# A linear-attention and feed-forward kernel on one core: new task lengths in its order planner, two small tiles moved to ScalarE, a ring of three, other PSUM banks at the end

## The chip, the cores and the metric

The kernel runs on one core of a Trainium2 chip. A core has four engines that compute: TensorE (PE, matmuls; the profile lists its weight loads apart as PEld), VectorE (DVE), ScalarE (ACT) and GpSimd (POOL). A fifth, SyncE (SP), issues the transfers (DMAs). Each engine works through its own queue strictly in the order in which the program was written, and waits at an instruction whose inputs or whose room are not there yet. The metric is the device time of one execution in microseconds (us); less is better.

## The reference

What is computed is a recurrence over 768 time steps, for 32 (batch, head) pairs with a state of 40 by 40, then a layer norm and a feed-forward block on its output:

```python
for t in range(S):                         # S = 768
    y[:, :, t] = einsum('bhd,bhde->bhe', rt, state)
    Sa = einsum('bhde,bhe->bhd', state, at)
    state_decay = state * wt[:, :, None, :] - einsum('bhd,bhe->bhde', Sa, bt)
    state = state_decay + einsum('bhd,bhe->bhde', vt, kt)
...
xn = (x - mu) / np.sqrt(var + 1e-06) * g_ln
ch = np.maximum(xn @ w_ch1, 0.0) @ w_ch2   # 320 -> 1280 -> 320
return x + ch
```

All of it is in float32.

## The kernel before

**Tiling.** The 768 steps are cut into 24 chunks of 32 steps (`NCH`, `C`). Inside a chunk the recurrence is written as matrices: a triangular system is set up (`prep`), its inverse is built (`invert` and `merge`), the state is carried to the next chunk (`chain`), and the chunk's output is formed (`post`). `norm` normalises a chunk's 128 output rows and transposes them; `moe` runs the feed-forward block over two chunks at a time (a pair, 256 rows). In `moe` the 1280 hidden units go in ten slices `f`: layer 1 of a slice is 8 matmuls of 256 columns into one PSUM bank (L794), ScalarE takes the rectified high part out into `hh` (L797), VectorE the remainder into `hl` (L799), and layer 2 is 6 matmuls of 320 columns that add to the pair's two output banks (L778). `weights` loads the feed-forward weights in pieces and converts each to a high and a low part, with work on ScalarE, VectorE (L671 to L674) and TensorE (L717, L718).

**The inverse.** The triangular blocks go through DRAM (`d_l`), come back one row per matrix (`yv`), and are inverted there by 14 pairs of small multiplications and additions (L425, L429): on VectorE for chunks 0 and 1, on GpSimd from chunk 2 on. The result goes through DRAM again (`d_h`) and comes back as `hv`. `merge(c)` multiplies `hv` twice by a column of 0 and 1 (`half`) into the tile `dg` (L444; block diagonals), on VectorE for chunks 0 and 1, on GpSimd after that, and two groups of matmuls (L452, L462) and a transposition (L472) make the full inverse `tt`, which `chain` needs (L531).

**The order of the work.** No line of the kernel issues work straight away. Each step is a task that is handed to the planner (`op`, `dma`, then `Plan.add`) with an engine, a length in us, a key (its priority, about the chunk's number), what it reads and writes, the PSUM banks it opens, and for transfers their KB. `Plan.order` then simulates the engines and goes on picking the task that can start soonest, on each engine the lowest key among those within 0.05 us, and issues the tasks in the order of the planned starts. The planned times are thrown away; only the order in each queue and the choice of banks stay. On the chip an engine waits if something planned to be there isn't.

The planner knows a few more things. `HOP` is added when a result passes between engines. A transfer goes through one pipe (`pipe`) at 200 KB per us, and the next is held until the pipe is at most `queue` us from free. On PE, `dense` tasks (the feed-forward block) and the other, `sparse` ones are alternated: after 2.9 us of sparse work (`SPARSE`) a dense task is wanted, and dense work goes on for at least 1.7 us (`DENSE`). Each PE task has a number of instruction records (`recs`); every 128 of them (`READ`) a fetch of 3.8 us (`FETCH`) must be through. Tasks with `lock=True` (scans and products on VectorE and GpSimd) are never planned at the same time.

PSUM has eight banks in three groups: A (four, the recurrence and the conversion of weights), H (two, layer 1, `norm`'s transposition and the first step of the conversion), M (two, the output of layer 2):

```python
with tc.manual_schedule():
    for t in P.order(dict(A=[0, 1, 2, 3], H=[4, 5], M=[6, 7])):
        t["fn"]()
```

`hh` and `hl` are rings of two tiles, so layer 1 of slice `f` may not be planned before layer 2 of slice `f - 2` is done (`room`, L796). Keys: `consts` makes `half` and `ones` (from the identity, L308 and L310) with key -60; `prep(0)` and `prep(1)` have -5.4 and -4.4, so those small operations come ahead of nearly all of `prep(0)` that is ready at the time.

Of the kernel before, what the change touches and what calls it, by code (L numbers as in the profile page):

```python
# [49 lines left out]
class Plan:  # L50


    HOP = 0.15
    SPARSE, DENSE = 2.9, 1.7
    READ, FETCH, STALL = 128, 3.8, 0.2
# [29 lines left out]
    def order(self, free):  # L85
# [13 lines left out]
        pipe, out, lock = 0.0, [], 0.0  # L99
# [19 lines left out]
        while len(out) < len(T):  # L119
            best = None  # L120
            for e, ns in ready.items():
# [17 lines left out]
                if best is None or s < best[0]:  # L139
                    best = s, n  # L140
# [7 lines left out]
            end = s + t["us"]  # L148
            if t["lock"]:
                lock = end  # L150
            if t["recs"]:
                read += t["recs"]
                if read >= self.READ:
                    read -= self.READ
                    at = end - t["us"] * read / t["recs"]
                    since = max(at, since + self.FETCH)
                    end += since - at
# [25 lines left out]
def body(ctx, tc, ea, eb, vr, rd, vt, w1, w1x_in, w2, gl, fe, fd, out):  # L183
# [62 lines left out]
    hh, hl = ring(2, "hh", 256, dt=F32R), ring(2, "hl", 256, dt=F32R)  # L246
# [18 lines left out]
    def dma(key, kb, rd, wr, to, of, us=0.4, queue=2.0):  # L265
# [4 lines left out]
    def consts():  # L270
# [40 lines left out]
        op("DVE", 1.5, -60, ["ident"], ["half", "ones"], f)  # L311
# [16 lines left out]
    def prep(c):  # L328
# [17 lines left out]
        op("DVE", 1.4, kp, W + [("start", h)], [("q", i)] + ([("go",)] if c == 0 else []), lambda: nc.vector.tensor_tensor_scan(  # L346
            out=flat(q[R])[:, ::-1], data0=t[R, n:0:-1], data1=flat(start[h][R])[:, ::-1], initial=0.0,
            op0=ALU.mult, op1=ALU.max), lock=True)
        op("DVE", 0.29, kp, [("q", i)], ["last"], lambda: nc.vector.reciprocal(
            out=last[R, :, 0:1], in_=q[R, :, 0:1]))  # L350
        op("DVE", 1.35, kp, W + ["last"], [("g", i)], lambda: nc.vector.tensor_tensor_scan(
            out=flat(g[R]), data0=t[R, 0:n], data1=flat(last[R]), initial=0.0, op0=ALU.mult, op1=ALU.max), lock=True)
        eng, e, us = ("DVE", nc.vector, 1.0) if c < EARLY else ("POOL", nc.gpsimd, 1.8)
        for hf, rs in enumerate(ROWS):
            if c >= XS:
                op("POOL", 0.6, kp - 0.3, (), [("x2k", x, 2 * hf), ("x2k", x, 2 * hf + 1)], lambda vs=slice(VROW[hf], VROW[hf] + C), hf=hf: nc.gpsimd.memset(
                    x2s[x][vs, hf, 0:512], 0.0))
            op(eng, 0.75 * us, kp, W + [("q", i)], [("x2a", x, hf)], lambda hf=hf, rs=rs: e.tensor_tensor(  # L358
# [6 lines left out]
        op(eng, 1.25 * us, kp, [("g", i)], K, lambda: e.tensor_tensor(  # L365
# [15 lines left out]
        for bb in range(2):  # L381
            m = 32 * j + 16 * bb
            dma(kp + 0.3, 150, [("gk", i)], [("d_l", s, 2 * j + bb)], d_l[s][m:m + 16].rearrange("m a t -> a m t"),
                gk[i][64 * bb + C:64 * bb + 64].rearrange("a (m t) -> a m t", t=C), 0.5)
        for hf in range(2):
            for bb in range(2):
                dma(kp + 0.4 + (1.0 if c < 2 else 0.0), 33, [("gk", i)], [("x2k", x, 2 * hf + bb)],
                    x2s[x][VROW[hf]:VROW[hf] + C, hf, 256 * bb:256 * bb + 256],
                    gk[i][64 * bb:64 * bb + C, 256 * hf:256 * hf + 256], 0.65)
# [10 lines left out]
        op("PE", 0.35, c - 1.8, ["qc", "ident"], [b], f, opens=[b], room=[("pi", c % KT)], recs=4)  # L400
        op("ACT", 0.45, c - 1.8, [b], [("pi", c % KT)], lambda b=b: nc.scalar.copy(
# [3 lines left out]
    def invert(s):  # L405
# [6 lines left out]
        eng, e, us = ("DVE", nc.vector, 0.54) if c0 < 2 else ("POOL", nc.gpsimd, 0.8)  # L412
# [3 lines left out]
        dma(k0, 131 * n // 32, L, Y, y[:, 0:1024], d_l[s].rearrange("m a t -> m (a t)"))  # L416
# [16 lines left out]
        dma(k0 + 0.4, 150 * n // 32, Y, [("d_h", s, 0)], d_h[s][:, :, B:3 * B].rearrange("a m t -> m a t"), rows[:, 0:B], 0.65)  # L433
        dma(k0 + 0.2, 150 * n // 32, L, [("d_h", s, 1)], d_h[s][:, :, 0:B].rearrange("a m t -> m a t"), d_l[s][:, B:C, 0:B], 0.65)

    def merge(c):
# [3 lines left out]
        dma(c - 1.3 - soon(c), 100, [("d_h", s, 0), ("d_h", s, 1)], [("hv", i)], hv[i],  # L440
            d_h[s][:, 32 * j:32 * j + 32].rearrange("a (g h) n -> g a (h n)", h=4), 0.6)
        eng, e = ("DVE", nc.vector) if c < 2 else ("POOL", nc.gpsimd)
        for x in range(2):
            op(eng, 0.25 if c < 2 else 0.4, c - 0.8 - soon(c), [("hv", i), "half"], [("dg", i)], lambda x=x: e.tensor_scalar(  # L444
                out=dg[i][:, :, :, x].rearrange("p y h t -> p h y t"),
# [553 lines left out]
```

## Time and profile before

| what | value |
|---|---|
| median of 3 runs | 575.66 us (572.37 to 577.28) |
| the profiled execution | 572.31 us |
| its span, first to last instruction | 570.2 us |
| mean granted TensorE clock | 0.969 |
| DMA over the span | 62.33 MB, 109 GB/s mean |

The span is what the profile shows; the profiled execution takes 2.1 us more than its span. In the tables of the profile, "idle before" is the time in which an engine did nothing ahead of an instruction, and the name behind the arrow is what ended the wait. "issue" there means that nothing the profile shows was waited for. "PEclk" is the granted clock of TensorE as a share of full speed. A window "A:B" is a stretch in us from the span's start. "x32" counts instructions.

### The profile page before, as it was taken

To read this page: it belongs to the slowest core of one execution; us is meant where nothing else is said; L and a number is where in the kernel's file an instruction comes from. 1 tells how busy PE (TensorE), PEld (TensorE's weight loads), DVE (VectorE), ACT (ScalarE), POOL (GpSimd) and SP (SyncE) were. 2 spreads that over 40 slices of the span, in tenths; PEclk is the share of its full clock that TensorE was granted. 3 is DMA by queue.
4 is the path that set the end of the run, shared out by engine and by line. 5 is a ranking of instruction groups with operands and counts; after the bars stand their busy time and mean duration, and the time that the engine had idled before them with its cause. 6 is when DMAs were issued, how large, how long until landed. Compare 5 with 4: busy or idle time off the path is not lost.

```text
span 570.2 us, 30783 instructions
## 1 busy us (share of the span) xinstructions
PE 504.1 (88%) x13462; PEld 452.9 (79%) x13462; DVE 404.0 (71%) x888; ACT 333.1 (58%) x848; POOL 304.1 (53%) x551
## 2 busy tenths in 40 slices
PE   2508787999999999999999999999999998999995
PEld 1406665798888898989888899899899897888995
DVE  7887897588638768767766774797884666778621
ACT  6538657674665765566556556666666656466321
POOL 9315277677284865864766836747838717200000
PEclk9999868699999999989999999999999999899999
DMA  6574665423533443443444344334434444333000
GB/s 165 130 203 126 173 184 160 117 79 109 130 86 102 121 126 86 107 114 89 102 131 103 89 114 110 103 101 110 126 81 108 115 100 115 100 108 95 3 24 28
DMA packets 80299, 62.33 MB, mean 109 GB/s; under 512 B 56224, under 2 KB 65440, under 8 KB 80160
## 3 DMA queue, kind: packets, MB, share of 16 engines
q1 hardware_dynamic: 80160, 60.31, 40.2%
q8 instruction: 107, 1.75, 1.3%
q14 instruction: 32, 0.26, 0.1%
HBM read 48.49 MB, written 9.44 MB: 102 GB/s over the span
## 4 chain that ended last, share of the span: by engine, by line
PE 58%; POOL 9%; issue 5%; DMA 4%; DVE 4%; ACT 3%; SPq 2%; POOLq 0%; DVEq 0%; ACTq 0%
PE bank L778 16%; PE bank L794 16%; POOL ytmp L425 3%; POOL yv L429 3%; PE bank L606 3%; PE bank L375 3%; PE bank L496 2%; PE bank L546 2%; PE bank L623 2%; PE bank L531 2%; PE bank L521 2%; PE bank L591 2%; PE bank L579 2%; SPq L266 1%; PE bank L472 1%
## 5 line engine op out<-in xcount | busy, mean ns | idle before, releaser
L778 PE MATMUL bank<-w,hh 128*128 128x320 f32 x480 | 116.5, 328 | 0.0
L794 PE MATMUL bank<-xh,w 128*128 128x256 f32 x480 | 107.9, 288 | 2.6 <-DVE hl L799 2.0
L797 ACT ACTIVATE hh<-bank 128x256 fp32r<-128x256 f32 x120 | 46.1, 384 | 96.8 <-PE bank L794 94.4
L799 DVE SCALAR_TENSOR_TENSOR hl<-bank,hh 128x256 fp32r<-128x256 f32 x120 | 50.1, 420 | 73.3 <-ACT hh L797 72.2
L794 PEld LDWEIGHTS bank<-xh,w 128*128 128x128 f32 x480 | 82.8, 190 | 4.3 <-DVE hl L799 2.4
L778 PEld LDWEIGHTS bank<-w,hh 128*128 128x128 f32 x480 | 76.6, 189 | 3.4
L778 PE MATMUL bank<-w,hl 128*128 128x320 f32 x240 | 74.6, 311 | 0.0
L365 POOL TENSOR_TENSOR bk<-bk,gE 104x1024 f32<-104x1024 f32 x22 | 50.9, 2313 | 32.7 <-DMA bk<-in_eb_dram 13.5
L794 PE MATMUL bank<-xl,w 128*128 128x256 f32 x240 | 67.6, 282 | 0.0
L358 POOL TENSOR_TENSOR x2s<-wa,qE 40x512 f32<-40x512 f32 x44 | 52.9, 1202 | 23.8 <-DVE qE L346 17.1
L425 POOL TENSOR_TENSOR ytmp<-yv 64x28 f32<-64x28 f32 (+6 forms) x154 | 55.5, 360 | 11.3
L429 POOL TENSOR_TENSOR yv<-yv,ytmp 64x28 f32<-64x28 f32 (+6 forms) x154 | 53.9, 350 | 12.1
L506 POOL MEMSET x5s<- 64x512 f32 x48 | 25.1, 523 | 48.3 <-PE bank L623 43.1
L501 ACT COPY xk<-bank 64x320 f32<-64x320 f32 x96 | 40.2, 419 | 17.7 <-PE bank L496 15.7
L612 DVE TENSOR_TENSOR x5s<-bank,mask 64x256 f32<-64x256 f32 x96 | 40.5, 422 | 13.6 <-PE bank L606 11.0
L794 PEld LDWEIGHTS bank<-xl,w 128*128 128x128 f32 x240 | 45.8, 191 | 0.0
L778 PEld LDWEIGHTS bank<-w,hl 128*128 128x128 f32 x240 | 45.6, 190 | 0.0
L535 ACT COPY x<-bank 32x320 f32<-32x320 f32 x96 | 40.1, 417 | 8.6 <-PE bank L531 7.2
L594 ACT COPY xk<-bank 40x320 f32<-40x320 f32 x96 | 40.2, 419 | 6.2 <-PE bank L591 4.3
L444 POOL TENSOR_SCALAR dg<-hv,half 128x128 f32<-128x128 f32 x44 | 29.6, 688 | 22.5 <-DMA hv<-d_h 22.5
L375 PE MATMUL bank<-x2s,bk 104*64 104x64 f32 x768 | 31.1, 240 | 11.4 <-issue 5.4
L475 ACT ACTIVATE tt<-bank,half 32x128 f32<-32x128 f32 x96 | 34.4, 358 | 10.6 <-PE bank L472 7.5
(136 smaller groups left out, 1130.9 us busy)
## 6 DMA issues: line engine op xcount, KB each, us to landing
wa<-in_ea_dram SPq DMA_DIRECT2D x48, 162.7 KB
bk<-in_eb_dram SPq DMA_DIRECT2D x48, 160.0 KB
vu<-in_vr_dram SPq DMA_DIRECT2D x48, 160.0 KB
wa<-in_ea_dram SPq DMA_DIRECT2D x24, 165.0 KB
x<-in_vt_dram SPq DMA_DIRECT2D x48, 80.0 KB
x5s<-in_rd_dram SPq DMA_DIRECT2D x48, 80.0 KB
out_dram<-ot SPq DMA_DIRECT2D x24, 160.0 KB
r<-in_w_dram SPq DMA_DIRECT2D x10, 320.0 KB
```

The lines of the kernel that those rows point to most:

```text
L358: op(eng, 0.75 * us, kp, W + [("q", i)], [("x2a", x, hf)], lambda hf=hf, rs=rs: e.tensor_tensor(out=x2s[x][rs, hf, 0:512].rearrange("p (h ...
L365: op(eng, 1.25 * us, kp, [("g", i)], K, lambda: e.tensor_tensor(out=kb, in0=kb, in1=g[R, :, 0:C].unsqueeze(2).broadcast_to([104, 16, 2, C] ...
L375: mm(pg[64 * bb:64 * bb + 64, :, h], lhsT=tb[R, 64 * p:64 * p + 64], rhs=x2s[x][R, :, 32 * p:32 * p + 32], start=True, stop=True)
L425: e.tensor_tensor(out=tv, in0=yb[:, :, j + 1:, j:j + 1].broadcast_to(S), in1=yb[:, :, j:j + 1, 0:j].broadcast_to(S), op=ALU.mult)
L429: e.tensor_tensor(out=v, in0=v, in1=tv, op=ALU.add)
L501: op("ACT", 0.45, c - 1.2 + 0.1 * bb, [bs[hf]], [X[hf]], lambda b=bs[hf], zs=zs, hf=hf, bb=bb: nc.scalar.copy(out=xk[i][zs, hf, 8 * bb:8 * ...
L594: op("ACT", 0.44, k + 0.35, [bs[hf]], [("ST", i)], lambda b=bs[hf], rs=rs, hf=hf, bb=bb: nc.scalar.copy(out=xk[i][rs, hf, 8 * bb:8 * bb + ...
L612: op("DVE", 0.46, k + 0.5, [b, "mask"], [("z", i)], lambda b=b, zs=zs, ps=ps, hf=hf, bb=bb: nc.vector.tensor_tensor(out=x5s[i][zs, hf, 8 * ...
L778: mm(bank_of(po[u])[:, 0:CH], lhsT=l[:, us], rhs=ws[f"w2_{f // 2}"][:, f % 2, x], start=f == 0 and n == 0, stop=f == 9 and n == 2)
L794: mm(ph, lhsT=l, rhs=r, start=n == 0, stop=n == 7)
L797: yield "ACT", 0.39, [phs[f]], [("hh", f % 2)], lambda f=f: nc.scalar.activation(out=hht[f % 2], in_=bank_of(phs[f])[:, 0:256], func=AF.Re ...
L799: yield "DVE", 0.46, [phs[f], ("hh", f % 2)], [("hl", f % 2)], lambda f=f: nc.vector.scalar_tensor_tensor(out=hlt[f % 2], in0=bank_of(phs[ ...
```

## The change

It has five parts.

1. **Lengths and rates of the planner.** Some forty task lengths are replaced by others, most within 10%: layer 1 from 1.0 to 1.03, layer 2 from 0.95 to 0.98, the scans from 1.4 and 1.35 to 1.28, the GpSimd products from 1.35 to 1.18 (L358), a converted slice of a weight from 1.5 to 1.56, the transfer of `d_l` from 150 to 113 KB, that of `vr` from 110 to 164. A PE task planned to start before 49.6 us now counts 1.8 times its length; after a planned gap of over 1.7 us on PE, tasks count 1.7 times for 3.4 us. The DMA pipe goes from 200 to 270 KB per us. `HOP` and `FETCH` are slightly smaller.
2. **Ties and locks.** Where two locked tasks on different engines could start at the same planned time, the one with the lower key is taken; before it was the engine listed first. GpSimd's `dg` products are now locked.
3. **The first diagonals.** In `merge(0)` and `merge(1)` the two products into `dg` are done by ScalarE. The products into `half` and `ones` get key -4.5 in place of -60.
4. **Rings of three.** `hh` and `hl` have three tiles each, so layer 1 of slice `f` needs layer 2 of slice `f - 3` to be done.
5. **Banks of the last pair.** The ten layer-1 results of the last pair of chunks go to group A in place of H.

```diff
-    HOP = 0.15
+    HOP, LAST = 0.13, 0.06
     SPARSE, DENSE = 2.9, 1.7
-    READ, FETCH, STALL = 128, 3.8, 0.2
+    READ, FETCH, STALL = 128, 3.75, 0.2
+    FIRST, COLD, WAIT, AFTER, LOW = 49.6, 1.8, 1.7, 3.4, 1.7
...
-                if best is None or s < best[0]:
+                if best is None or s < best[0] or s == best[0] and T[n]["lock"] and T[best[1]]["lock"] and T[n]["key"] < T[best[1]]["key"]:
                     best = s, n
...
-            end = s + t["us"]
+            us = t["us"]
+            if t["eng"] == "PE":
+                if s - engines["PE"] > self.WAIT:
+                    cold = max(cold, s + self.AFTER)
+                us *= self.COLD if s < self.FIRST else self.LOW if s < cold else 1.0
+            end = s + us
...
-            done = end
+            done = end + (self.LAST if t["eng"] == "PE" else 0.0)
             if t["eng"] == "SP":
-                pipe = max(pipe, end + 1.3) + t["kb"] / 200.0
-                done = pipe + 0.7 + t["late"]
+                pipe = max(pipe, s + 1.4) + t["kb"] / 270.0
+                done = pipe + 1.0 + t["late"]
...
-    hh, hl = ring(2, "hh", 256, dt=F32R), ring(2, "hl", 256, dt=F32R)
+    hh, hl = ring(3, "hh", 256, dt=F32R), ring(3, "hl", 256, dt=F32R)
...
-        op("DVE", 1.5, -60, ["ident"], ["half", "ones"], f)
+        op("DVE", 1.3, -4.5, ["ident"], ["half", "ones"], f)
...
+        sc = c < 2
         for x in range(2):
-            op(eng, 0.25 if c < 2 else 0.4, c - 0.8 - soon(c), [("hv", i), "half"], [("dg", i)], lambda x=x: e.tensor_scalar(
...
+            if sc:
+                op("ACT", 0.35, c - 0.8 - soon(c), [("hv", i), "half"], [("dg", i)], lambda x=x, to=to, of=of: nc.scalar.mul(
+                    out=to, in_=of, mul=half[:, x:x + 1]))
+            else:
+                op("POOL", 0.6, c - 0.8 - soon(c), [("hv", i), "half"], [("dg", i)], lambda x=x, to=to, of=of: nc.gpsimd.tensor_scalar(
+                    out=to, in0=of, scalar1=half[:, x:x + 1], scalar2=None, op0=ALU.mult), lock=True)
...
-            yield "PE", 1.0, X + W, [phs[f]], fn, [phs[f]], [(a, f % 2) for a in ("hh", "hl")]
+            yield "PE", 1.03, X + W, [phs[f]], fn, [phs[f]], [(a, f % R) for a in ("hh", "hl")]
...
-                    [out[2 * g], out[2 * g + 1]], bank_of, [Bank("M"), Bank("M")], [Bank("H") for _ in range(10)]):
+                    [out[2 * g], out[2 * g + 1]], bank_of, [Bank("M"), Bank("M")], [Bank("H" if c + 1 < NCH else "A") for _ in range(10)]):
```

The other changed lines replace a length or a number of KB. The number of operations and transfers, and what each computes, stays as it was, but for the four products that go from VectorE to ScalarE.

More of the change, by code (lines that the diff above doesn't have):

```diff
@@ L718, in f @@
                     mm(at(h), lhsT=minus, rhs=ws[tag][:, h, 0], start=False, stop=True)
-                op("PE", 0.75, key, M + W + ["ident", "minus", "diag"], [one[h]], f,
+                op("PE", 0.8, key, M + W + ["ident", "minus", "diag"], [one[h]], f,
                    opens=[one[h]] if k == 2 or h == 0 else (), recs=3)
             if k == 1:
-                op("ACT", 0.63, key, [one[0]], W, lambda: nc.scalar.copy(
+                op("ACT", 0.59, key, [one[0]], W, lambda: nc.scalar.copy(
                     out=ws[tag][:, :, 1], in_=bank[one[0].at].rearrange("p (k n) -> p k n", k=2)))
@@ L725, in pair @@
                 for h in range(2):
-                    op("ACT", 0.45, key, [one[h]], W, lambda h=h: nc.scalar.copy(out=ws[tag][:, h, 1], in_=at(h)))
+                    op("ACT", 0.43, key, [one[h]], W, lambda h=h: nc.scalar.copy(out=ws[tag][:, h, 1], in_=at(h)))
         last(0.0)
```

114 lines of the change are left out of this document (57 added, 57 removed).

## The prediction, made before the changed kernel had run

> **What bounds the kernel now.** I read the table of stages first, the busy time of each engine in six windows, because the page's shares mix a start, a long middle and an end.
>
> ```profile
> core 0: us, PE busy (x) PEld busy (x) DVE busy (x) ACT busy (x) POOL busy (x), PEclk, DMA share, GB/s
> 0.00:42.00 42.00, 11.45 (x253) 9.87 (x257) 35.48 (x104) 21.24 (x41) 20.24 (x42) 1.00 0.63 163
> 42.00:57.00 15.00, 13.23 (x430) 10.32 (x422) 11.36 (x14) 11.65 (x30) 9.06 (x6) 1.00 0.48 138
> 57.00:114.00 57.00, 46.13 (x906) 36.14 (x904) 44.61 (x90) 37.47 (x93) 34.15 (x64) 0.76 0.60 158
> 114.00:535.00 421.00, 404.77 (x11675) 368.44 (x11675) 301.62 (x653) 256.20 (x668) 240.60 (x442) 0.99 0.40 104
> 535.00:563.36 28.36, 28.34 (x218) 28.00 (x216) 10.31 (x28) 6.57 (x18) 0.00 (x0) 1.00 0.04 13
> 563.36:570.20 6.84, 0.19 (x2) 0.09 (x2) 0.66 (x3) 0.00 (x0) 0.00 (x0) 0.87 0.17 58
> ```
>
> From 114 us on TensorE (PE) is the bound: 404.77 of 421 us busy, then 28.34 of 28.36. Its work there is the same in any order, so a new order can win only the idle 16.2 us and what the clock loses. Before 42 us VectorE sets the pace (35.48 of 42), with PE waiting. Between 57 and 114 us nothing is full: PE idles 10.9 us, and its clock is granted at 0.76. Where that clock is lost:
>
> ```profile
> 77.50:87.50 10.00, 9.35 (x82) 7.16 (x81) 9.17 (x23) 6.82 (x17) 8.20 (x24) 0.52 0.67 181
> 98.00:111.50 13.50, 13.36 (x237) 9.79 (x234) 7.47 (x13) 8.10 (x21) 8.68 (x15) 0.52 0.57 155
> 244.50:248.50 4.00, 4.00 (x79) 3.73 (x79) 2.21 (x5) 2.80 (x8) 3.24 (x5) 0.61 0.58 155
> ```
>
> Two stretches at half clock early on; a short one later, right behind an idle 1.62 us (the 243.70 row below). Half clock doubles a group: the 32 matmuls of L375 take 1.98 us at 78.13 and 1.15 at 443.39.
>
> ```profile
> 75.16 0.69 PE L623 MATMUL bank<-xk,x5s 128*32 128x40 f32 x50 [1.65 <-issue]
> 78.13 1.98 PE L375 MATMUL bank<-x2s,bk 104*64 104x64 f32 x32
> 97.25 1.86 PE L375 MATMUL bank<-x2s,bk 104*64 104x64 f32 x32 [1.57 <-POOL bk L365]
> 243.70 0.34 PE L496 MATMUL bank<-ident,bk 40*64 40x40 f32 x9 [1.62 <-issue]
> 443.39 1.15 PE L375 MATMUL bank<-x2s,bk 104*64 104x64 f32 x32 [0.56 <-POOL bk L365]
> ```
>
> So a PE gap of about 1.6 us costs more than itself: 244.50 to 248.50 at 0.61 lost 4 x 0.39 = 1.6 us of work; the stretches from 77.5 and 98 lost 10 x 0.48 = 4.8 and 13.5 x 0.48 = 6.5, as far as PE was then the bound.
>
> **Step 1, the first diagonals go to ScalarE.**
>
> ```profile
> 38.93 1.26 DVE L346 TENSOR_TENSOR_SCAN qE<-wa,start 104x528 f32<-104x528 f32 x1
> 40.21 1.39 DVE L444 TENSOR_SCALAR dg<-hv,half 128x128 f32<-128x128 f32 x2
> 46.36 2.98 DVE L444 TENSOR_SCALAR dg<-hv,half 128x128 f32<-128x128 f32 x2
> 45.14 2.99 POOL L365 TENSOR_TENSOR bk<-bk,gE 104x1024 f32<-104x1024 f32 x1 [2.34 <-issue]
> 41.70 0.62 PE L452 MATMUL bank<-hv,dg 32*32 32x16 f32 x32 [14.80 <-DVE dg L444]
> 51.69 0.44 PE L452 MATMUL bank<-hv,dg 32*32 32x16 f32 x32
> 35.11 0.70 SPq L266 DMA_DIRECT2D hv<-d_h x1
> 209.40 4.30 DMA hv<-d_h
> L639 ACT ACTIVATE diag<-ident,gt 128x128 f32<-128x128 f32 x2 | 0.7, 394 | 0.0
> ```
>
> The row of L452 shows PE idle for 14.80 us until `dg(0)`. Removed from VectorE: 1.39 + 2.98 = 4.37 us. Added to ScalarE: four products like L639's, the same shape with a scale from a column: 4 x 0.394 = 1.58 us, the two of a chunk in 0.79. For `dg(0)`: `hv` was issued at 35.11, and by a later transfer's 4.30 us from there on it lands at about 35.81 + 4.30 = 40.1, just when VectorE starts. So only 1.39 - 0.79 = 0.6 us is won there, provided ScalarE's copy of `qc`, 0.63 us long and ready with the scan's end at 40.19, goes second; if first, the win is nothing. For `dg(1)`, 2.98 - 0.79 = 2.2 us, but PE reaches that L452 only at 51.69, behind the state of chunk 0, so this can be zero unless the planner moves it up. Besides, VectorE has 4.37 us less in a stretch that it fills. Bounds 0 to 4.4 us; I take 0.6 + 2.2 = **2.8**, because the early stage is a chain through VectorE and PE in turn, and `dg(1)` gates chunk 1.
>
> The 2.98 us overlap a GpSimd product (45.14 to 48.13), the 1.39 one at 40.27. The Trainium skill (SBUF — State Buffer, section "SBUF: two separate sides") says that VectorE and GpSimd share a port pair that one holds for a whole instruction, and that ScalarE never waits for it. By that rule the move takes the collision away; the two rows agree, and the sum already has it.
>
> **Step 2, `half` and `ones` with a later key.**
>
> ```profile
> 7.47 0.14 DVE L308 TENSOR_TENSOR ones<-ident 32x16 f32<-32x16 f32 x1
> 8.81 0.26 DVE L349 RECIPROCAL last<-qE 104x16 f32<-104x16 f32 x1
> 15.00 0.69 DVE L378 TENSOR_TENSOR gk<-bank,sign 128x512 f32<-128x512 f32 x1 [0.67 <-PE bank L375]
> 21.80 0.69 DVE L378 TENSOR_TENSOR gk<-bank,sign 128x512 f32<-128x512 f32 x1 [0.54 <-PE bank L375]
> ```
>
> They stand on VectorE from 7.47 to 8.8, ahead of all of chunk 0's products; moved back, chunk 0 is 1.3 us earlier. VectorE's work before 40 us is the same, so only its idle time can shrink: 0.67 + 0.54 = 1.2 us. Bounds 0 to 1.2; I take **0.7**. ScalarE's `lt` copies, which read `ones`, become ready later and hold nothing before `merge`.
>
> **Step 3, rings of three and step 5, other banks.**
>
> ```profile
> L794 PE MATMUL bank<-xh,w 128*128 128x256 f32 x410 | 92.7, 289 | 2.6 <-DVE hl L799 2.0 <-DVE xl L766 0.6
> ```
>
> Between 114 and 535 us layer 1 waited for `hl` 2.0 us in all. That wait can be the ring or the H bank that L799 frees; a third tile doesn't add a bank. Bounds 0 to 2.0; I take **0.5**. The last pair's banks: the window from 535 us has 0.02 us of idle PE, so there is nothing to fill, and I take 0; bounds 0 and, if copies of group A are in the way, one L799 wait like those above, 1 us lost.
>
> **Step 4, lengths, rates and ties: only order.** Nothing becomes shorter on the chip. What a better order can take away are PE's waits:
>
> ```profile
> PE bank L397 <- ACT qc L398: 2.0, 1, 2.0
> PE bank L623 <- issue: 1.7, 1, 1.7
> PE bank L375 <- POOL bk L365: 1.6, 1, 1.6
> PE bank L496 <- issue: 2.9, 2, 1.6
> PE bank L531 <- issue: 2.8, 2, 1.4
> PE bank L452 <- POOL dg L444: 1.5, 2, 1.0
> PE bank L531 <- ACT tt L475: 1.1, 1, 1.1
> ```
>
> The first three lie in 57:114, the rest in 114:535. In the middle, "issue" waits are the larger part: 2.9 and 2.8 of 16.2 us alone; the planner's fetch length moves only from 3.8 to 3.75, so I leave them. Waits for an engine add up to 7.2 us of the 10.9 early (nine rows, 2.0 to 0.2) and to 7.4 us of the 16.2 later (nine rows, 2.0 to 0.2). Changes of length are mostly under 10%; the large ones are true to the trace (half-speed PE at the start; GpSimd's `dg` 0.6 us in place of 0.4). The tie rule keeps GpSimd's inversions from going ahead of VectorE's scans in the plan. Ends: all 14.6 us won, or as much lost by new gaps; I take a fifth won, **3.0 us**, near nothing because the middle is already 96% busy.
>
> **The sum.** 572.3 (the profiled execution, whose span is 570.2) - 2.8 - 0.7 - 0.5 - 3.0 = 565.3, **565 us**. The profiled execution lies 3.4 us under the median, 575.66, so against that median the forecast is 1.9% faster. Within 1% means 569.9 to 581.4; a 1% change is about what a measurement of this kernel can tell from none, as three runs of it span 572.37 to 577.28.
>
> **The rivals.**
>
> *A, the half clock goes.* If the new order closes the gaps that end at 75.16 and 97.25, the stretches behind them stay at full clock: 4.8 + 6.5 = 11.3 us more, 565.3 - 11.3 = 554 us. For it: the planner now prices such gaps. Against: it picks the task that can start soonest either way and does not seek to avoid a gap.
>
> The Trainium skill (TensorE: Matmul & The Clock Gate, section "What's actually happening") says that the clock is gated by free-running windows of about 3.4 us that do not reset with the kernel. By that rule a gap of 1.6 us halves the clock or not by where it falls, so a shift of 3 us at the start may add or remove a stretch by luck. The trace agrees that one 1.62 us gap had it and shows no second one to compare.
>
> *B, the gain is absorbed.* The 4.4 us of VectorE work were beside the loads of the weights, and PE then waits for those. For it: no engine is full between 57 and 114 us, and VectorE waited up to 5.9 us there for a step of the conversion. Steps 1 to 3 give about 1 us and the order nothing: 571 to 572 us.
>
> ```profile
> DVE bank L671 <- ACT bank L666: 7.9, 3, 5.9
> ```
>
> *C, slower: weight loads ahead of `hv`.* At 270 KB per us in the plan, SP is let on earlier and more 320 KB pieces can be queued before the small transfers that gate the first two merges.
>
> ```profile
> 39.96 1.28 SPq L266 DMA_DIRECT2D r<-in_w_dram  x2
> 43.38 0.65 SPq L266 DMA_DIRECT2D hv<-d_h  x1
> r<-in_w_dram SPq DMA_DIRECT2D x10, 320.0 KB
> ```
>
> The early windows moved 163 to 181 GB/s; at an estimated 180 a piece takes 1.8 us. Three more ahead of each `hv` make 2 x 3 x 1.8 = 10.8 us, and a PE that has cooled loses another 1.6 as at 244.5; with steps 2 and 3 and a third of step 4 kept, 572.3 - 0.7 - 0.5 - 1.0 + 10.8 + 1.6 = 582 us. It decides from two pieces each on: 7.2 + 1.6 = 8.8 us is over the 7.0 us of the sum. Against: `hv(1)` already has two such pieces ahead of it, and keys still put `hv` first when both are ready.
>
> **How the numbers follow.** Forecast (560 to 570 us) 0.45, A 0.13, B 0.27, C 0.15. The time is the forecast's, 565. Cutting A's and C's far halves leaves 552 to 580 as the range. Faster by over 1% (under 569.9): nearly all of the forecast and A, 0.55. Within 1%: B and the near part of C, 0.31. Slower: 0.14.
>
> **What would show it.** Step 1: L452's first group before 41.1 us, its second well before 51.69, no `dg` on VectorE, and four products near 0.39 us on ScalarE. Step 2: L349 at about 7.5 us, VectorE's 0.67 us wait gone. Step 3: fewer waits of L794 for `hl`. Step 5: PE still without a gap in its last 28 us. Step 4: less than 16.2 us of PE idle in the middle. A shows as a granted clock near 1 where it was 0.52; C as a first L452 later than 41.70. I am wrong altogether if the middle's PE idle time grows by more than the start wins, or if PE's busy time itself changes by several us at full clock.

## The result, and the profile after

The changed kernel takes 595.06 us (median of four runs: 587.76, 593.98, 596.14 and one of 897.98, which the ratio leaves out; the median of the other three is 593.98). The kernel before, run beside it, took 574.77. The ratio is 1.032, with a 95% interval of 1.0258 to 1.0381: slower, where 565 us and a gain were forecast.

The profiled execution took 596.14 us, its span is 594.2, 24.0 more than before; the two medians are 20.3 apart, so this pair of executions shows the loss somewhat large. The table of stages of the kernel after, with the columns of the first table of the prediction:

```profile
core 0: us, PE busy (x) PEld busy (x) DVE busy (x) ACT busy (x) POOL busy (x), PEclk, DMA share, GB/s
0.00:42.00 42.00, 15.13 (x242) 11.82 (x242) 32.81 (x87) 22.45 (x44) 20.00 (x42) 1.00 0.66 177
42.00:57.00 15.00, 10.87 (x267) 8.51 (x267) 13.92 (x32) 10.52 (x27) 8.43 (x4) 1.00 0.60 169
57.00:114.00 57.00, 50.52 (x1137) 40.59 (x1136) 44.28 (x91) 40.01 (x98) 27.50 (x49) 0.85 0.53 135
114.00:553.00 439.00, 406.65 (x11565) 366.40 (x11564) 296.69 (x651) 254.24 (x665) 252.51 (x456) 0.98 0.39 100
553.00:587.35 34.35, 33.56 (x255) 32.91 (x253) 10.12 (x25) 7.26 (x19) 0.00 (x0) 1.00 0.03 10
587.35:594.20 6.85, 0.19 (x2) 0.09 (x2) 0.36 (x2) 0.00 (x0) 0.00 (x0) 0.66 0.19 60
```

The time went into the long middle and nowhere else. From 114 us to the end of PE's work it is 587.35 - 114 = 473.35 us, where it was 449.36: 24.0 us, the whole difference. PE idles 32.35 + 0.79 = 33.14 us of it, where it idled 16.25: 16.9 us. Between 57 and 114 us the kernel after is the better one: 6.5 us of idle PE for 10.9, and a granted clock of 0.85 for 0.76.

A second part is the clock. These windows of the kernel after are all its stretches at half clock behind 114 us:

```profile
156.10:159.50 3.40, 3.40 (x38) 3.17 (x35) 0.69 (x1) 0.84 (x2) 2.85 (x8) 0.50 0.29 52
197.10:200.50 3.40, 3.40 (x51) 3.31 (x38) 0.71 (x1) 0.46 (x2) 2.85 (x8) 0.50 0.02 5
292.70:296.10 3.40, 3.40 (x93) 3.21 (x89) 2.88 (x6) 1.14 (x3) 2.72 (x4) 0.51 0.59 163
398.50:401.90 3.40, 3.40 (x34) 3.17 (x36) 0.00 (x0) 0.74 (x3) 2.68 (x10) 0.50 0.35 103
521.30:524.70 3.40, 3.18 (x25) 3.09 (x26) 1.94 (x4) 1.99 (x6) 0.00 (x0) 0.51 0.31 93
```

Five stretches of 3.4 us at half speed lose 5 x 1.7 = 8.5 us of work; before there were two, 3.4 us. The 5.1 us more and the 16.9 us of idle time make 22.0 of the 24.0.

What does PE wait for? The waits of the kernel after between 114 and 553 us (in all, times, longest, in us):

```profile
PE bank L383 <- POOL bk L373: 3.5, 4, 1.4
PE bank L636 <- ACT xk L607: 2.8, 1, 2.8
PE bank L475 <- issue: 2.5, 2, 1.7
PE bank L774 <- DVE xn L766: 1.9, 1, 1.9
PE bank L465 <- POOL dg L458: 1.8, 2, 1.1
PE bank L509 <- ACT x L548: 1.7, 2, 1.1
PE bank L405 <- DVE xt L640: 1.6, 1, 1.6
```

These are the first seven rows. Summed over all of them, waits for another engine come to 21.1 us, where the step on order in the prediction counted 7.4, and the "issue" waits to 10.8 us, where there were 8.6. So nearly the whole growth is PE waiting for another engine, a little at each of many places; layer 1's wait for `hl` is no longer among them. No engine is much fuller than before (VectorE 296.69 us in 439, before 301.62 in 421; GpSimd 252.51, before 240.60, 57.5% for 57.1%). So the engines are not too slow, they are late. The share of each engine in the chain that ended last, first before, then after:

```profile
PE 58%; POOL 9%; issue 5%; DMA 4%; DVE 4%; ACT 3%; SPq 2%; POOLq 0%; DVEq 0%; ACTq 0%
```

```profile
PE 54%; POOL 13%; DMA 10%; DVE 9%; issue 6%; SPq 4%; ACT 3%; POOLq 0%; ACTq 0%; DVEq 0%
```

Transfers went from 4% to 10%. Their steps of 1 us and more on that chain between 80 and 500 us, each with its start (its issue) and its length up to the landing, before (beside the 209.40 row of the prediction):

```profile
95.40 4.33 DMA r<-in_w_dram
150.07 3.64 DMA yv<-d_l
184.22 4.41 DMA bk<-in_eb_dram
323.04 1.84 DMA x2s<-gk
475.58 3.44 DMA wa<-in_ea_dram
```

and after:

```profile
89.94 5.50 DMA d_h<-yv
95.50 3.56 DMA hv<-d_h
110.94 3.68 DMA yv<-d_l
127.29 4.71 DMA d_h<-yv
132.02 2.86 DMA hv<-d_h
150.13 3.39 DMA d_h<-d_l
269.14 4.24 DMA yv<-d_l
436.31 5.09 DMA yv<-d_l
460.40 4.74 DMA wa<-in_ea_dram
480.08 3.71 DMA d_h<-d_l
```

The planner's landing of the same transfers, from the start of the issue and with the pipe empty, follows from its lines. For `d_h<-yv` of two chunks it was 0.65 + 1.3 + 300/200 + 0.7 = 4.15 us and is 1.4 + 226/270 + 1.0 = 3.24; for `d_h<-d_l` 4.15 and 3.14; for `yv` 3.71 and 3.37; for `hv` 3.10 and 2.83; for `wa` 3.24 and 3.02. The chain rows are the late ones by selection. Each of the ten after is later than the new plan has it in an empty pipe, `d_h<-yv` by 1.5 and 2.3 us; but six of them are later than the old plan had it too, so these rows alone don't say how much slack is enough. The four transfers from `d_l` to `hv`, one after the other, come to 12.3 us in the plan, where they came to 14.2. If instructions that need them are put in front of others, an engine that takes its queue in order stands there. That is a reading of the trace; the experiments test it.

### The profile page after: what moved, and what is told of

The parts are those of the page before. It is cut to its first block, busy times and chain, and to the rows that moved or that the text cites. A ratio compares the mean times of both kernels' runs of the same rounds, so it can differ in the third digit from the quotient of the medians.

```text
span 594.2 us, 30771 instructions
## 1 busy us (share of the span) xinstructions
PE 516.9 (87%) x13462; PEld 460.3 (77%) x13462; DVE 398.2 (67%) x884; ACT 334.5 (56%) x852; POOL 308.4 (52%) x551
## 4 chain that ended last, share of the span: by engine, by line
PE 54%; POOL 13%; DMA 10%; DVE 9%; issue 6%; SPq 4%; ACT 3%; POOLq 0%; ACTq 0%; DVEq 0%
PE bank L792 14%; PE bank L808 13%; POOL ytmp L433 5%; POOL yv L437 5%; SPq L274 4%; PE bank L619 3%; PE bank L383 3%; DMA wa<-in_ea_dram 3%; DMA yv<-d_l 2%; PE bank L534 2%; PE bank L636 2%; PE bank L509 2%; PE bank L604 2%; PE bank L544 2%; DMA d_h<-yv 2%
## 5 line engine op out<-in xcount | busy, mean ns | idle before, releaser
L792 PE MATMUL bank<-w,hh 128*128 128x320 f32 x480 | 118.4, 332 | 1.2 <-issue 0.8
L808 PE MATMUL bank<-xh,w 128*128 128x256 f32 x480 | 109.3, 290 | 1.0 <-issue 1.0
L792 PEld LDWEIGHTS bank<-w,hh 128*128 128x128 f32 x480 | 77.8, 192 | 4.3 <-ACT hh L811 0.7
L366 POOL TENSOR_TENSOR x2s<-wa,qE 40x512 f32<-40x512 f32 x44 | 58.4, 1327 | 21.0 <-DVE qE L354 19.5
L373 POOL TENSOR_TENSOR bk<-bk,gE 104x1024 f32<-104x1024 f32 x22 | 50.7, 2303 | 31.3 <-DMA bk<-in_eb_dram 14.2
L625 DVE TENSOR_TENSOR x5s<-bank,mask 64x256 f32<-64x256 f32 x96 | 40.5, 422 | 18.6 <-PE bank L619 14.5
L514 ACT COPY xk<-bank 64x320 f32<-64x320 f32 x96 | 40.1, 418 | 9.1 <-PE bank L509 7.0
L364 POOL MEMSET x2s<- 32x512 f32 x40 | 21.0, 526 | 45.6 <-PE bank L534 35.7
L607 ACT COPY xk<-bank 40x320 f32<-40x320 f32 x96 | 40.1, 418 | 7.9 <-PE bank L604 6.1
L383 PE MATMUL bank<-x2s,bk 104*64 104x64 f32 x768 | 32.5, 246 | 11.8 <-POOL bk L373 3.5
L383 PEld LDWEIGHTS bank<-x2s,bk 104*64 104x64 f32 x768 | 29.0, 157 | 15.2 <-POOL bk L373 4.4
```

The source lines that it names most:

```text
L366: op(eng, 0.68 if c < EARLY else 1.18, kp, W + [("q", i)], [("x2a", x, hf)], lambda hf=hf, rs=rs: e.tensor_tensor(out=x2s[x][rs, hf, 0:512 ...
L373: op(eng, 1.23 if c < EARLY else 2.25, kp, [("g", i)], K, lambda: e.tensor_tensor(out=kb, in0=kb, in1=g[R, :, 0:C].unsqueeze(2).broadcast_ ...
L383: mm(pg[64 * bb:64 * bb + 64, :, h], lhsT=tb[R, 64 * p:64 * p + 64], rhs=x2s[x][R, :, 32 * p:32 * p + 32], start=True, stop=True)
L514: op("ACT", 0.42, c - 1.2 + 0.1 * bb, [bs[hf]], [X[hf]], lambda b=bs[hf], zs=zs, hf=hf, bb=bb: nc.scalar.copy(out=xk[i][zs, hf, 8 * bb:8 * ...
L607: op("ACT", 0.42, k + 0.35, [bs[hf]], [("ST", i)], lambda b=bs[hf], rs=rs, hf=hf, bb=bb: nc.scalar.copy(out=xk[i][rs, hf, 8 * bb:8 * bb + ...
L625: op("DVE", 0.43, k + 0.5, [b, "mask"], [("z", i)], lambda b=b, zs=zs, ps=ps, hf=hf, bb=bb: nc.vector.tensor_tensor(out=x5s[i][zs, hf, 8 * ...
```

## The experiments

The expectations name the theories by letters. Theory P: the plan's new numbers leave it without slack, so PE stands in front of inputs that come late. It is split later: theory D puts it down to the numbers for transfers, which make the plan expect data too early; theory E to the lengths of the engines' work; theory K to the clock model; theory T to the tie rule and the lock. Theory R: the new structure, the ring above all, costs the time. Theory L: any new order costs this much by luck. Theory A: every part costs a little. Theory X: the pipe's rate has a best value near 200. Ratios are to the kernel before, run on the same chip.

### Halves of the change

The parts 3, 4 and 5 alone on the kernel before, all lengths, rates and ties as before (`e2_struct_only`):

```diff
-    hh, hl = ring(2, "hh", 256, dt=F32R), ring(2, "hl", 256, dt=F32R)
+    hh, hl = ring(3, "hh", 256, dt=F32R), ring(3, "hl", 256, dt=F32R)
...
-        op("DVE", 1.5, -60, ["ident"], ["half", "ones"], f)
+        op("DVE", 1.5, -4.5, ["ident"], ["half", "ones"], f)
...
+                op("ACT", 0.35, c - 0.8 - soon(c), [("hv", i), "half"], [("dg", i)], lambda x=x, to=to, of=of: nc.scalar.mul(
+                    out=to, in_=of, mul=half[:, x:x + 1]))
```

> The kernel before with only the diagonals on ScalarE, the later key, the rings of three and the last pair's banks; every length, rate and tie rule as before. Theory P: at or below the kernel before, 566 to 575 us, idle PE in the middle near 16 us. Theory R: slower, 585 to 597 us. Theory L: anywhere from 565 to 595 us.

569.41 us, 0.993 [0.9877, 0.9983]. The other half, parts 1 and 2 alone (`e3_lengths_only`):

```diff
-                pipe = max(pipe, end + 1.3) + t["kb"] / 200.0
-                done = pipe + 0.7 + t["late"]
+                pipe = max(pipe, s + 1.4) + t["kb"] / 270.0
+                done = pipe + 1.0 + t["late"]
...
-            yield "PE", 1.0, X + W, [phs[f]], fn, [phs[f]], [(a, f % 2) for a in ("hh", "hl")]
+            yield "PE", 1.03, X + W, [phs[f]], fn, [phs[f]], [(a, f % 2) for a in ("hh", "hl")]
```

> The kernel before with only the planner's new lengths, rates, clock model, ties and locks. Theory P: 588 to 600 us, PE idle in the middle 28 us or more. Theory R: 568 to 578 us. Theory L: anywhere from 570 to 600 us.

603.34 us, 1.0515 [1.0444, 1.0585]. And the kernel after with rings of two again (`e1_after_ring2`):

```diff
-    hh, hl = ring(3, "hh", 256, dt=F32R), ring(3, "hl", 256, dt=F32R)
+    hh, hl = ring(2, "hh", 256, dt=F32R), ring(2, "hl", 256, dt=F32R)
```

> The changed kernel with rings of two again, all else as changed. Theory P (the new lengths and rates leave the plan without slack, so PE stands in front of inputs that come late): about as slow as the changed kernel, 588 to 598 us, idle PE time between 114 and 570 us near 32 us. Theory R (the third tile lets the plan put layer 1 too far ahead): back to 570 to 578 us, idle near 16 us. Theory L (any edit draws a new order, and the time of an order is largely luck): anywhere from 570 to 600 us.

605.78 us, 1.0562 [1.049, 1.0634]. Both are slower than any theory had them. The structure is a small gain, the plan's numbers are the loss, and the ring of three hides a part of it: without the ring the same plan costs about 605.8 - 595.1 = 10.7 us more by the medians, 2.4% by the ratios. The middle window of the half with the structure, then of the half with the lengths:

```profile
114.00:535.00 421.00, 407.18 (x11589) 368.15 (x11584) 295.83 (x651) 255.65 (x669) 244.07 (x454) 1.00 0.40 104
```

```profile
114.00:563.00 449.00, 417.40 (x11602) 374.29 (x11602) 295.42 (x653) 255.66 (x667) 245.51 (x455) 0.95 0.37 98
```

13.8 us of idle PE and full clock in the one, 31.6 us and 0.95 in the other, at nearly the same number of matmuls. Theory R falls.

### Is it luck of the order?

The kernel before with one length moved that means nothing (`e4_hop14`), and the kernel after likewise (`e17_after_hop12`):

```diff
-    HOP = 0.15
+    HOP = 0.14
```

> The kernel before with one number of the plan moved by 0.01 us (HOP 0.15 to 0.14), which says nothing new about the chip. Theories P and R: within 1% of the kernel before, 570 to 581 us. Theory L: off by several us either way, 565 to 595 us, with another order on PE almost from the start.

```diff
-    HOP, LAST = 0.13, 0.06
+    HOP, LAST = 0.12, 0.06
```

> The changed kernel with one number of the plan moved by 0.01 us (HOP 0.13 to 0.12), which says nothing new about the chip but draws another order. Slack theory: still 588 to 605 us. Theory L (the changed kernel drew an unlucky order): 570 to 586 us.

576.85 us, 1.0053 [0.9978, 1.0128], and 593.95 us, 1.037 [1.0262, 1.0478]. A redrawn order moves either kernel by half a per cent, inside the intervals, not by three. Theory L falls as the cause of the whole loss. Two edits are a small sample of the luck: parts that differ by 1% can't be told from a redrawn order, and perhaps not those that differ by 2%.

### Which of the new numbers

All on the kernel of `e2_struct_only`. First every new transfer number (`e5_s_dma`):

```diff
-                pipe = max(pipe, end + 1.3) + t["kb"] / 200.0
-                done = pipe + 0.7 + t["late"]
+                pipe = max(pipe, s + 1.4) + t["kb"] / 270.0
+                done = pipe + 1.0 + t["late"]
...
-    def dma(key, kb, rd, wr, to, of, us=0.4, queue=2.0):
+    def dma(key, kb, rd, wr, to, of, us=0.34, queue=2.0):
...
-        dma(k0 + 0.4, 150 * n // 32, Y, [("d_h", s, 0)], d_h[s][:, :, B:3 * B].rearrange("a m t -> m a t"), rows[:, 0:B], 0.65)
+        dma(k0 + 0.4, 113 * n // 32, Y, [("d_h", s, 0)], d_h[s][:, :, B:3 * B].rearrange("a m t -> m a t"), rows[:, 0:B], 0.65)
```

> The version of e2 (569.4 us) with only the planner's numbers for transfers as in the changed kernel: pipe at 270 in place of 200 KB per us, issue lengths and KB. Theory D (the faster pipe makes the plan count on loads that are not there yet): most of the 26 us between e2 and the changed kernel, 585 to 598 us. Theory K (the clock model), T (ties and locks) and E (lengths of the engines' work): 566 to 574 us.

594.23 us, 1.0334 [1.025, 1.0418]. Then the engines' lengths with `HOP`, `LAST` and `FETCH` (`e6_s_len`):

```diff
-    HOP = 0.15
+    HOP, LAST = 0.13, 0.06
...
-        op("DVE", 1.4, kp, W + [("start", h)], [("q", i)] + ([("go",)] if c == 0 else []), lambda: nc.vector.tensor_tensor_scan(
+        op("DVE", 1.28, kp, W + [("start", h)], [("q", i)] + ([("go",)] if c == 0 else []), lambda: nc.vector.tensor_tensor_scan(
```

> The version of e2 with only the lengths of the engines' tasks and of the hops between engines as in the changed kernel. Theory E (the old lengths were longer than the chip's on ScalarE and GpSimd, and that slack kept inputs ahead of PE): 585 to 598 us, PE idle in the middle 28 us or more. Theories D, K and T: 566 to 574 us.

578.28 us, 1.003 [0.9988, 1.0072]. The clock model (`e7_s_clock`):

```diff
+                if s - engines["PE"] > self.WAIT:
+                    cold = max(cold, s + self.AFTER)
+                us *= self.COLD if s < self.FIRST else self.LOW if s < cold else 1.0
```

> The version of e2 with only the clock model (PE tasks 1.8 times as long before 49.6 us, 1.7 times after a planned gap over 1.7 us). Theory K (it moves the early work of VectorE and PE to another order that PE then waits for): 580 to 598 us, lost mostly before 114 us. Theories D, E and T: 565 to 573 us, since it acts on the first 50 us alone.

570.65 us, 0.9929 [0.9883, 0.9975]. The tie rule and the lock on `dg` (`e8_s_tie`):

```diff
-                if best is None or s < best[0]:
+                if best is None or s < best[0] or s == best[0] and T[n]["lock"] and T[best[1]]["lock"] and T[n]["key"] < T[best[1]]["key"]:
```

> The version of e2 with only the tie rule and the lock on GpSimd's dg. Theory T (scans now go ahead of GpSimd's inversions in the plan, the inversions come late, and PE waits for merges): 580 to 598 us, with waits of L452's group for GpSimd. Theories D, E and K: 566 to 573 us.

578.68 us, 1.014 [1.008, 1.0201]. And the reverse of `e5_s_dma`: the kernel after with every transfer number of before (`e9_after_olddma`):

```diff
-                pipe = max(pipe, s + 1.4) + t["kb"] / 270.0
-                done = pipe + 1.0 + t["late"]
+                pipe = max(pipe, end + 1.3) + t["kb"] / 200.0
+                done = pipe + 0.7 + t["late"]
```

> The changed kernel with the planner's transfer numbers of before (pipe at 200, its waits, issue lengths, KB); all other parts of the change stay. Theory D (the transfer numbers cost it): 570 to 580 us, PE idle in the middle 20 us or less. Theory A (the parts each cost something, only their sum is 20 us): 582 to 590 us. Theory L (luck of the order): not to be told, 570 to 605 us.

575.46 us, 1.0014 [0.9971, 1.0058]. The transfer numbers are enough to make the loss (`e5_s_dma`), and it is gone without them (`e9_after_olddma`). The middle of that last kernel, 19.9 us of idle PE at full clock:

```profile
114.00:535.00 421.00, 401.12 (x11532) 362.39 (x11530) 295.48 (x654) 256.38 (x669) 231.69 (x426) 1.00 0.39 103
```

Theories E, K and T fall as the main cause; the clock model costs nothing. Against `e2_struct_only` the tie rule costs 2% and the lengths 1%, the second within reach of a redrawn order. The parts do not add up: 4.0% for the transfer numbers, 2.1% and 1.0% make 7.1%, where all together cost 3.9%, and `e9_after_olddma`, with tie rule, lengths and clock model, lies only 0.8% above `e2_struct_only`. So single costs of this size are not to be trusted one by one.

### Which transfer number

The rate alone, on the kernel of `e2_struct_only`, set to 150, 235 and 270 (`e10_rate150`, `e11_rate235`, `e12_rate270`):

```diff
-                pipe = max(pipe, end + 1.3) + t["kb"] / 200.0
+                pipe = max(pipe, end + 1.3) + t["kb"] / 270.0
```

> The version of e2 with the one number of the pipe at 150 KB per us in place of 200. Theory D as a matter of slack (a plan that believes in slower loads issues them earlier in its order, and PE meets fewer late ones): no slower than e2, 562 to 570 us. Theory X (the rate has a best value near 200, too slow holds loads back): 573 to 590 us. Theory L: anywhere from 565 to 600 us.

> The version of e2 with the one number of the pipe at 235 KB per us. Theory D by the rate alone: between e2 and e5, 575 to 585 us. If the rate isn't the cause but the latency, the issue lengths or the KB are: 566 to 573 us.

> The version of e2 with the one number of the pipe at 270 KB per us, all other transfer numbers as before. Theory D by the rate alone: as e5, 588 to 598 us, and slower than the run at 235. If the latency, the issue lengths or the KB are the cause: 566 to 575 us.

584.81 us, 1.0146 [1.0088, 1.0203]; 576.44, 1.0023 [0.9965, 1.0081]; 578.0, 1.0019 [0.9958, 1.008]. The rate alone is not the cause: 576.44 lies in the range that theory D gave, but 270 is no slower than 235, as it had to be, and is far from 588. And a pipe that is planned too slow costs as well. That goes against the simple form of the slack theory, which had 562 to 570 us for the rate of 150, and fits theory X; this run plans every landing later and costs 2% against `e2_struct_only`.

From the kernel after, one group of numbers at a time set as before: the two lines of the pipe (`e13_pipe_old`, the diff of `e9_after_olddma` and nothing else), the KB (`e14_kb_old`) and the lengths of SP's issues (`e15_us_old`):

> The changed kernel with only the pipe's two lines as before (start 1.3 us behind the issue's end, 200 KB per us, 0.7 us to land); KB and issue lengths stay as changed. If the pipe's lines are the cause: 573 to 583 us. If KB or issue lengths are: 588 to 600 us.

```diff
-        dma(c - 0.6, 164, (), [("vT", i, hf), ("uT", i)], vu[i][rs], vr[c, hf])
+        dma(c - 0.6, 110, (), [("vT", i, hf), ("uT", i)], vu[i][rs], vr[c, hf])
```

> The changed kernel with only the KB of the five kinds of transfer as before. If the smaller KB of the inverse's way through DRAM (113 and 100 for 150) are the cause, by a plan that expects its parts too soon: 573 to 583 us. If not: 588 to 600 us.

```diff
-    def dma(key, kb, rd, wr, to, of, us=0.34, queue=2.0):
+    def dma(key, kb, rd, wr, to, of, us=0.4, queue=2.0):
```

> The changed kernel with only the issue lengths of the transfers as before (0.4 for 0.34 and the like). If a plan that fills SP's queue too densely is the cause: 573 to 583 us. If not: 588 to 600 us.

579.47 us, 1.0108 [1.0063, 1.0153]; 593.74, 1.0288 [1.0208, 1.0369]; 588.11, 1.0214 [1.0161, 1.0268]. The pipe's lines take back two thirds of the loss, the KB nothing that can be measured, the issues perhaps a third.

The run that bears most on the landings keeps every new number, rate and KB included, and only lets each transfer land 1 us later in the plan (`e16_late1`):

```diff
-                done = pipe + 1.0 + t["late"]
+                done = pipe + 2.0 + t["late"]
```

> The changed kernel with one number moved: every transfer is planned to land 1 us later (2.0 for 1.0), rate, KB and issue lengths as changed. Slack theory (the plan counts on landings sooner than the chip gives them): 573 to 583 us, PE idle in the middle 20 us or less. If the order on SP or the rate matters, not the landing: 588 to 600 us.

579.22 us, 1.0095 [1.0056, 1.0133]: one constant, 595.1 - 579.2 = 15.8 us, or 2.2% by the two ratios. The time is in the range of the slack theory; the idle time of 20 us or less that it wanted is not reached, as the middle below shows. The same on the old numbers, in the kernel of `e2_struct_only` (`e18_s_late1`):

```diff
-                done = pipe + 0.7 + t["late"]
+                done = pipe + 1.7 + t["late"]
```

> The version of e2 with every transfer planned to land 1 us later (1.7 for 0.7), all else as in e2. If slack in landings helps without bound: 560 to 569 us. If the numbers of before were about enough, and more only delays tasks in the plan: 570 to 585 us.

571.31 us (565.26 to 578.26), too spread for a ratio: no gain and no loss to be seen. So the slack of the old numbers seems to have been enough, and that of the new ones, 0.2 to 1.0 us less on each step of the inverse's way through DRAM, was not.

The middle of `e16_late1`: 22.9 us of idle PE in 426, where the kernel after has 32.35 in 439. Its profiled execution, the longest of its ten (583.58 us), has a span 12.3 us shorter than that of the kernel after. From 114 us to the end of PE's work it idles 9.4 us less and loses 3.4 us more by the clock (the table below); the other 6.3 us are work already done by 114 us, 1723 matmuls for 1646. So the gaps are part of what the constant brings, not all.

```profile
114.00:540.00 426.00, 403.11 (x11435) 365.06 (x11432) 294.53 (x636) 251.57 (x658) 238.00 (x438) 0.97 0.39 102
```

A queue in which such waits can be seen directly is SP's own. Its waits for transfers, first before, then after (in all, times, longest, in us, over the whole span):

```profile
SPq L266 <- DMA wa<-in_ea_dram: 7.4, 9, 2.8
SPq L266 <- DMA d_h<-yv: 4.2, 4, 2.1
```

```profile
SPq L274 <- DMA d_h<-yv: 15.8, 12, 4.0
SPq L274 <- DMA wa<-in_ea_dram: 11.9, 12, 3.5
```

The transfer that reads `d_h` (`hv`) is put into SP's queue for the time at which the plan has `d_h` written. Where that is later, SP stands, and every transfer behind it in the queue is issued later. The row of `d_h<-yv` is 14.4 to 23.6 us in the five kernels with all new transfer numbers (after, `e1_after_ring2`, `e3_lengths_only`, `e5_s_dma`, `e17_after_hop12`) and 2.9 to 12.7 in all others. It is a sign and not the whole path: `e14_kb_old` has 9.1 us there and takes 593.74.

### All runs side by side

For the profiled execution of each: PE's idle time from 114 us to 6.85 us before the end of the span, the clock lost there (one minus the granted clock, summed over windows of 1 us), and the span.

| run | idle | clock lost | sum | span |
|---|---|---|---|---|
| e2_struct_only | 14.1 | 1.7 | 15.8 | 567.0 |
| e18_s_late1 | 14.8 | 3.4 | 18.2 | 566.3 |
| before | 16.2 | 3.4 | 19.6 | 570.2 |
| e9_after_olddma | 20.8 | 0.0 | 20.8 | 574.8 |
| e7_s_clock | 17.2 | 5.1 | 22.3 | 565.9 |
| e8_s_tie, e12_rate270 | 16.6, 18.2 | 10.2, 8.6 | 26.8, 26.8 | 576.7, 577.0 |
| e6_s_len, e11_rate235 | 18.6, 16.6 | 10.0, 12.0 | 28.6, 28.6 | 580.5, 572.1 |
| e4_hop14, e10_rate150 | 20.2, 21.1 | 8.5, 8.5 | 28.7, 29.6 | 578.4, 585.8 |
| e13_pipe_old | 25.0 | 6.8 | 31.8 | 576.7 |
| e16_late1 | 23.7 | 11.9 | 35.6 | 581.9 |
| e15_us_old | 27.7 | 8.7 | 36.4 | 588.0 |
| e5_s_dma | 25.4 | 13.6 | 39.0 | 590.5 |
| e14_kb_old | 26.8 | 13.6 | 40.4 | 591.7 |
| after | 33.1 | 8.5 | 41.6 | 594.2 |
| e17_after_hop12 | 32.5 | 13.7 | 46.2 | 595.6 |
| e3_lengths_only | 31.7 | 23.9 | 55.6 | 601.8 |
| e1_after_ring2 | 36.1 | 22.2 | 58.3 | 600.8 |

On the whole the span follows the sum, over a range of some 40 us, with a scatter of several us: the gaps and the half clock are the larger part of the loss in nearly every variant that is slower than the kernel before (in `e9_after_olddma` only 1.2 of 4.6 us). The share of transfers in the chain doesn't sort the versions so well: it is 6% in `e2_struct_only`, the fastest by the median, and 8% in `e16_late1`, and with the old numbers too landings come late there (in `e2_struct_only` four of `hv` after 3.60 to 4.46 us, planned at 3.10 in an empty pipe). That the late landings make the gaps is therefore shown by the edits of the plan's numbers, and not by the chain.

Two versions beat both kernels: the structure alone (`e2_struct_only`, 569.41 us) and the structure with the clock model (`e7_s_clock`, 570.65), both at 0.993 of the kernel before.

## Why the prediction was wrong, point by point

**Step 4 is the step that failed.** It said "only order", called the large changes of length "true to the trace", and put 3.0 us of gain between ends of 14.6 us. Measured alone it is 1.0515 (`e3_lengths_only`); on top of the rest it takes 569.4 to 595.1 us, 25.7 us by the medians (22 by the ratios), outside the ends. Two errors are in it. The lengths looked at were those of engines; the landings of transfers, the two lines that did it, were never set against the trace, though the chain had rows for them (4.30 us for an `hv` that the new plan lands after 2.83). And the price was bounded by PE's existing waits, as if a poorer order could only lengthen those once; it made new ones at many places (waits for another engine behind 114 us went from 7.4 to 21.1 us), and a gap can cost 1.7 us of clock besides. The clause that would make the prediction "wrong altogether", more idle PE in the middle than the start wins, is what happened: 16.9 us.

**Steps 1, 2, 3 and 5: the sum held, by luck.** They stood in the sum with 2.8 + 0.7 + 0.5 + 0 = 4.0 us; `e2_struct_only` gives 574.47 x 0.007 = 4.0 us, by its interval 1 to 7 us. But the largest term, step 1, won nothing where it was forecast to, so the agreement is luck. The first merges of the kernel after, on ScalarE, PE and SP:

```profile
43.30 0.69 ACT L455 ACTIVATE dg<-hv,half 128x128 f32<-128x128 f32 x2 [2.43 <-DMA hv<-d_h]
44.04 0.62 PE L465 MATMUL bank<-hv,dg 32*32 32x16 f32 x32 [2.21 <-ACT dg L455]
58.82 0.62 PE L465 MATMUL bank<-hv,dg 32*32 32x16 f32 x32
33.66 0.33 SPq L274 DMA_DIRECT2D d_h<-yv  x1
35.40 1.16 SPq L274 DMA_DIRECT2D r<-in_w_dram  x2
38.77 0.70 SPq L274 DMA_DIRECT2D hv<-d_h  x1
```

Step 1: a pair of products takes 0.69 us, where 0.79 was worked out. It starts 3.1 us later than VectorE's did at 40.21, as `hv(0)` is issued at 38.77 in place of 35.11. The transfer before it on the inverse's way, `d_h<-yv`, was issued at 33.66, before at 31.95, and SP stood 1.7 us for its landing; two pieces of weights had been issued in between. The prediction also counted the 4.30 us of its model row from the end of the issue, where the row counts from the start: by it `hv(0)` lands at 39.4 and not at 40.1. So the first group comes at 44.04, not before 41.1, and the second at 58.82, not well before 51.69. In `e2_struct_only`, with the old lengths, it is no earlier than before (41.70) either:

```profile
42.31 0.63 PE L457 MATMUL bank<-hv,dg 32*32 32x16 f32 x32 [13.45 <-ACT dg L447]
```

The gain of `e2_struct_only` lies in PE's idle time and clock behind 57 us: 7.4 and 14.1 us of idle PE for 10.9 and 16.2, while before 57 it idles 34.0 for 32.3.

Step 2: with `half` out of the way, the reciprocal forecast at 7.5 us starts at 8.74 (8.81 before), since `wa` lands later; only the 0.67 us wait ahead of `gk` is gone. The late landing took the place of the work that was moved. In `e2_struct_only` it does start at 7.64, as forecast, and the first `gk` at 13.85 for 15.00; but the second starts at 23.76 for 21.80, so the lead is lost there too.

```profile
7.45 1.26 DVE L354 TENSOR_TENSOR_SCAN qE<-wa,start 104x528 f32<-104x528 f32 x1 [2.42 <-DMA wa<-in_ea_dram]
8.74 0.26 DVE L357 RECIPROCAL last<-qE 104x16 f32<-104x16 f32 x1
15.53 0.67 DVE L386 TENSOR_TENSOR gk<-bank,sign 128x512 f32<-128x512 f32 x1
```

Step 3: the ring was priced at 0.5 us from the waits that the old order had. In `e2_struct_only` the wait for `hl` falls from 2.0 to 0.3 us, as the step had it; the ring alone on the old plan was not run. For the new plan 0.5 is too small: there the ring is worth some 10.7 us. Why it is, that layer 1 can be ordered further ahead of a late layer 2, is argued, not shown. Step 5: nothing won, as said; the tail's 0.79 us of idle PE, where there was 0.02, lies within the 1 us that the step allowed for.

**The sum and two readings.** The 565 us start from the profiled execution, 572.3, and are compared with the median, 575.66; of the forecast 1.9%, 0.6 is only the distance of the two. And the two rows of L375, 1.98 and 1.15 us, show a group 1.7 times as long at half clock, not doubled.

**The rivals.** Rival A came in part: between 57 and 114 us the clock rose from 0.76 to 0.85; but new half-clock stretches came in the middle. The clock's rule, cited there from the Trainium skill (TensorE: Matmul & The Clock Gate, "What's actually happening"), agrees in the length of each stretch, 3.4 us. But the Trainium skill has the clock fall there after a whole idle window of about 3.4 us. A gap of 1.6 us can't fill one, so the prediction took more from the rule than it says; the trace does show falls behind such gaps (the last section). Rival B isn't what happened: there was a loss, and in `e2_struct_only`, without the new lengths, the gain was not absorbed. Rival C named the right part of the plan, the pipe, and its sign of recognition is there: a first L452 (now L465) later than 41.70. Its place was wrong: the start had caught up by 114 us, by the count of matmuls (242 + 267 + 1137 = 1646 by then in its table of stages, 1589 in that of before), and the loss came from landings all along the middle, which C did not speak of. At 0.14 for slower, the chance was too low for a change that replaces every number a static order is built on.

**What stays open.** How the loss divides between queues is not settled. SP waits more for `d_h<-yv` (4.2 us in all before, 15.8 after), but `e16_late1` still has 11.9 us there. Why the rate of 270 alone costs 0.9% against `e2_struct_only`, and the pipe's two lines together 2.1% (`e13_pipe_old` against after), is open too; `s + 1.4` in place of `end + 1.3` wasn't tried alone. The kernel after with the pipe's lines as before (`e13_pipe_old`) is still 1% slower than the kernel before, and which of the remaining numbers does that is within what a redrawn order does. Two of the 24.0 us of the middle are neither idle time nor clock: PE is busy for that much longer at full clock behind 114 us (431.7 us for 429.7), and why is not known.

## What to carry to other kernels

In an order planned ahead for queues that run in order, a planned landing needs slack: here 1 us more on each was worth some 2% of the time with the tight numbers and cost nothing that could be seen with the loose ones (`e18_s_late1`). Slack by a slower planned pipe is another matter: it cost 2% (`e10_rate150`). Replace such numbers group by group, engines' lengths apart from landings, and redraw the order several times with meaningless edits to learn how much of a difference is luck. The price of a changed order isn't bounded by the waits of the old one.

## What the runs showed of the hardware

- Stretches of half clock follow PE gaps that are shorter than the stretches: in the kernel after no PE wait between 114 and 553 us is longer than 2.8 us, most are under 2, and there are five stretches of 3.4 us at 0.50. In the 3.4 us ahead of each, PE is busy for 1.05 to 2.78 us; but not every such gap is followed by one.
- The five stretches start at 156.1, 197.1, 292.7, 398.5 and 521.3 us, which is 12, 28, 31 and 36 times 3.41 us from one to the next. So where a gap falls on this grid seems to bear on whether it costs clock.
- Equal transfers land at quite different times: `d_h<-yv` on the chain took 5.50 and 4.71 us, `yv<-d_l` 3.64, 3.68, 4.24 and 5.09. The Trainium skill (DMA: Bandwidth & Descriptors, "🔬 Latency and other measured facts") gives 0.2 us of access latency to DRAM on average and 2 us at high load; the spread here, 1.45 us between equal `yv` loads, is of that size, but no run shows that load is its cause.
- The same work in a redrawn order, with nothing else changed, differed by half a per cent by the ratios, inside the intervals (`e4_hop14`, `e17_after_hop12`).
